# Rows gathered seven tiles ahead instead of three, and the eight PSUM buffers shared out anew

## The chip, the cores and the metric

The kernel runs on one core of one Trainium2 chip. The metric is the device time of one launch in microseconds (us); the median of three runs is given. The engines are PE (TensorE matmul), PEld (its weight loads), DVE (VectorE), ACT (ScalarE), POOL (GpSimd) and SP (SyncE, which here only starts DMAs). "Granted clock" is the share of full speed that PE was given: 1.00 is 2.4 GHz, 0.50 is 1.2 GHz.

## The reference

Linear attention with an RMS norm gives x (2304 tokens of 512), a top-1 mixture of eight experts follows, then a dense two-layer network.

```
kv = einsum('bhsd,bhse->bhde', k, v);  out = einsum('bhsd,bhde->bhse', q, kv)
x  = out / sqrt(mean(out*out) + 1e-6) * g_norm            # 2304 x 512
e  = argmax(x @ w_gate)                                   # one expert of 8 per token
y[token] = gate_w * (relu(x @ w1[e]) @ w2[e])             # 512 -> 1024 -> 512
h  = y @ w_in;  g = where(h > 0, h, exp(min(h, 0)) - 1);  out = g @ w_out   # 512 -> 2048 -> 512
```

## The kernel before, in words

The attention part writes the rows of x to a DRAM buffer (`x_dram`, 528 floats a row: 512 values and 16 scales), and works out `ids`, the order of the tokens sorted by expert. Experts are taken in rank order, the largest first; rank r works on a window of `WIN[r]` sorted tokens (352 for rank 0).

**Rows.** The sorted tokens form 18 tiles of 128 rows. For each tile a, POOL starts an indirect DMA (`gather`, line 494: 128 rows of 2112 bytes, 270 KB) into a row buffer `xg`; DVE scales the rows in place (`place_scale`, line 500); PE turns them with four 128x128 transposes into the PSUM tile `pt` (`place_turn`, line 507); ACT copies `pt` into `xT` (line 508). There are three row buffers (`XG = 3`), so the gather of tile a+3 is started behind the turn of tile a, and one `pt` buffer (`ps_x`).

**First window.** Tiles 0 to 2 are turned into the four `acc` buffers and become the split operands `xh`, `xl` of rank 0 at once (`first_window`, lines 561 to 571).

**Steps.** `step(u)` handles one eighth of an expert (8 steps a rank, 64 in all): it starts the weight loads of unit u+3 on SP (lines 532, 533, 256 KB each), runs the first-layer products h(u) (`expert_h`, 12 matmuls into `ph`, lines 587 to 589), then the second-layer products y(u-1) (`expert_y`, 12 matmuls into `acc`), and splits the weights of unit u+2 into a high and a low part (line 480 on ACT; line 483, in rank 0 `w1l` on POOL and `w2l` on DVE). From `ph`, ACT makes `hh` (line 606) and DVE `hl` (line 607).

Rank 0 also has to turn tiles 3 to 17, because rank 1 may start anywhere: `QUOTA[u]` tiles are turned in step u, one between h(u) and y(u-1), the others behind y(u-1); at step 5 all that are left are turned. Behind each step's turns `place_ahead(2)` scales the next two tiles. In steps 5 and 6 the window of rank 1 is made (`window`, lines 582, 583).

The program is issued in written order in this part (`tc.manual_schedule()`), so each engine's queue has the order of the code, and an instruction that waits holds up what stands behind it on its engine. `ps_h` holds the first-layer products `ph`, three buffers, in the expert part and in the dense network behind it (96 steps there: ACT reads `ph` twice over at lines 864 and 865, DVE makes `g` at line 867).

Of the kernel before, what the change touches and what calls it, by code (L numbers as in the profile page):

```python
# [9 lines left out]
F32 = mybir.dt.float32  # L10
# [7 lines left out]
PSUM = bass.MemoryType.PSUM  # L18
DRAM = bass.MemoryType.DRAM

P = 128
B, H, S, D = 4, 8, 576, 64
N, C = B * S, H * D
NT = N // P
# [17 lines left out]
def block_kernel(ctx, tc, qT, k, v, g_norm, w_gate, w1, w2, w_in, w_out, out, cap, **_):  # L42
    nc = tc.nc

    keep = ctx.enter_context(tc.tile_pool(name="keep", bufs=1))
    ids = keep.tile([P, NT], U32, name="ids")
# [7 lines left out]
    x_dram = dram.tile([N, C + 2 * H], F32, name="x_dram")  # L54
# [50 lines left out]
    with ExitStack() as actx:  # L105
# [30 lines left out]
        for b in range(B):  # L136
            t = ap1.tile([P, NP, KA], F32, name=f"kva{b}")
# [122 lines left out]
        def step(c, n=1):  # L260
            for _ in range(n):
                next(c)
# [200 lines left out]
    xw = ctx.enter_context(tc.tile_pool(name="xw", bufs=2, reuse_waits="tile"))  # L463
# [1 line left out]
    wst = ctx.enter_context(tc.tile_pool(name="wst", bufs=2, reuse_waits="tile"))  # L465
    ring = ctx.enter_context(tc.tile_pool(name="ring", bufs=7, reuse_waits="tile"))
    ps_a = ctx.enter_context(tc.tile_pool(name="ps_a", bufs=4, space=PSUM, reuse_waits="tile"))
    ps_h = ctx.enter_context(tc.tile_pool(name="ps_h", bufs=3, space=PSUM, reuse_waits="tile"))
    ps_x = ctx.enter_context(tc.tile_pool(name="ps_x", bufs=1, space=PSUM, reuse_waits="tile"))
    xctx = ExitStack()  # L470
    xp = xctx.enter_context(tc.tile_pool(name="xp", bufs=1, reuse_waits="tile"))
    xT = xp.tile([P, NP, NS], F32, name="xT")
# [12 lines left out]
    def ring_tiles():  # L485
        return [ring.tile([P, C], F32R, name=n) for n in ("w1h", "w1l", "w2h", "w2l")]

    XG = 3
    xg_t = {}

    def gather(a):
        if a < NT:
            xg_t[a] = wst.tile([P, C + 2 * H], F32, name="xg", tag="w64", bufs=XG)
            return nc.gpsimd.indirect_dma_start(out=xg_t[a], out_offset=None, in_=x_dram,
                                         in_offset=bass.IndirectOffsetOnAxis(ap=ids[:, a:a + 1], axis=0))

    def place_scale(a):
        xg = xg_t[a]
        v = xg[:, 0:C].rearrange("p (h d) -> p h d", h=H)
        nc.vector.scalar_tensor_tensor(out=v, in0=v, scalar=used[:, a:a + 1], in1=xg[:, C:C + H].to_broadcast([P, H, D]),  # L500
                                       op0=ALU.mult, op1=ALU.mult)

    def place_turn(a):
        xg = xg_t.pop(a)
        pt = ps_x.tile([P, NP, P], F32, name="pt")
        for j in range(NP):
            nc.tensor.transpose(pt[:, j], xg[:, j * P:(j + 1) * P], ident)
        nc.scalar.activation(xT[:, :, a * P:(a + 1) * P], pt, AF.Copy, scale=g_col)
        gather(a + XG)

    offs, eids = {}, {}

# [2 lines left out]
    def load_regs(r):  # L515
        with ExitStack() as behind:
            for i in mark.values():
                behind.enter_context(tc.issue_after(i.ins))
            eids[r] = reg(0, r, [SP_E], 0, E - 1)
            offs[r] = reg(1, r, [ACT_E, DVE_E], 0, off_max(r)) if r else 0  # L520
# [3 lines left out]
    def expert_load(u):  # L524
        if u >= NU:
            return
        r, fc = divmod(u, NF)
        if fc == 0:
            load_regs(r)
        a1 = wst.tile([P, C], F32, name="a1", tag="a", bufs=AB)  # L530
        a2 = wst.tile([P, C], F32, name="a2", tag="a", bufs=AB)
        first = nc.sync.dma_start(out=a1, in_=w1[bass.ds(eids[r], 1), fc].rearrange("o p c -> (o p) c"))
        mark["sp"] = nc.sync.dma_start(out=a2, in_=w2[bass.ds(eids[r], 1), fc].rearrange("o p c -> (o p) c"))
        wstage[u] = (a1, a2)
        return first

    def expert_split(u, engine=nc.gpsimd):
        if u >= NU:
            return
        w = ring_tiles()  # L540
        a1, a2 = wstage.pop(u)
        split_hi(w[0:2], a1)
        mark["act"] = split_hi(w[2:4], a2)
        split_lo(w[0:2], a1, engine)
        mark["dve"] = split_lo(w[2:4], a2, nc.vector)
        wtiles[u] = w
# [3 lines left out]
    def first_window():  # L550

        W = WIN[0]
        xh = xw.tile([P, NP, WIN[0]], F32R, name="xh")
        xl = xw.tile([P, NP, WIN[0]], F32R, name="xl")
        pts, ws = [], []
        for a in range(need[0]):
            place_scale(a)
            xg = xg_t.pop(a)
            pt = ps_a.tile([P, NP, P], F32, name="pt", tag="acc")
            for j in range(NP):  # L560
                nc.tensor.transpose(pt[:, j], xg[:, j * P:(j + 1) * P], ident)
            w = slice(a * P, min(W, (a + 1) * P))
            nc.scalar.activation(xh[:, :, w], pt[:, :, :w.stop - w.start], AF.Copy, scale=g_col)
            gather(a + XG)
            pts.append(pt)
            ws.append(w)
        for pt, w in zip(pts, ws):
            nc.vector.scalar_tensor_tensor(out=xl[:, :, w], in0=pt[:, :, :w.stop - w.start], scalar=g_col, in1=xh[:, :, w].bitcast(F32),
                                           op0=ALU.mult, op1=ALU.subtract)
        for a, pt in enumerate(pts):  # L570
            nc.scalar.activation(xT[:, :, a * P:(a + 1) * P], pt, AF.Copy, scale=g_col)
        xwin[0] = (xh, xl)
        placed["s"] = placed["t"] = need[0]
# [19 lines left out]
    def expert_h(u):  # L593
        r, fc = divmod(u, NF)
        W = WIN[r]
        w1h, w1l = wtiles[u][0:2]
        xh, xl = xwin[r]
        ph = ps_h.tile([P, C], F32, name="ph")

        for w in [slice(a, min(W, a + P)) for a in range(0, W, P)] if u < 0 else [slice(0, W)]:  # L600
            for j in range(NP):
                c = slice(j * P, (j + 1) * P)
                three(ph[:, w], (w1h[:, c], w1l[:, c]), (xh[:, j, w], xl[:, j, w]), j == 0, j == NP - 1)
        hh = hp.tile([P, WIN[0]], F32R, name="hh")
        hl = hp.tile([P, WIN[0]], F32R, name="hl")
        nc.scalar.activation(hh[:, :W], ph[:, :W], AF.Relu)  # L606
        nc.vector.scalar_tensor_tensor(out=hl[:, :W], in0=ph[:, :W], scalar=0.0, in1=hh[:, :W].bitcast(F32),
                                       op0=ALU.max, op1=ALU.subtract)
        hid[u] = (hh, hl)
# [25 lines left out]
    class Prep:  # L635
# [5 lines left out]
        def load(self):  # L641
            src = (w_in, w_out)[self.half][self.u]
            if wide:
                self.st = wst.tile([P, 2 * C], I32, name="w64", bufs=XG)
                nc.sync.dma_start(out=self.st, in_=src.bitcast(I32))
# [103 lines left out]
    def place_ahead(n):  # L749
        while placed["s"] < min(placed["t"] + n, NT):  # L750
            place_scale(placed["s"])
            placed["s"] += 1

    def place(n, ahead):

        while placed["t"] < min(n, NT):
            while placed["s"] < min(placed["t"] + 1, NT):
                place_scale(placed["s"])
                placed["s"] += 1
            place_turn(placed["t"])  # L760
            placed["t"] += 1
        place_ahead(ahead)
# [22 lines left out]
    APART = 4 * NF + 4  # L785
    FIRST = NF + 1

    QUOTA = (1, 2, 2, 3, 2, 2, 3, 0)

    def step(u):  # L790
        r, fc = divmod(u, NF)
# [6 lines left out]
        if u < NU:  # L798
            expert_h(u)
        q = QUOTA[u] if u < NF else 2 if more else 0  # L800
        if q:
# [23 lines left out]
    with tc.manual_schedule():  # L825
        expert_load(0)
        expert_load(1)
        gathers = [gather(a) for a in range(XG)]
        expert_split(0, nc.vector)
        expert_split(1, nc.vector)  # L830
        first_window()
        tc.add_manual_dep(expert_load(2).ins, gathers[1].ins.name, mybir.DependencyInfo(mybir.DependencyClass.Sync, mybir.DependencyReason.DATA),
                          reason="rows before weights")
        place_ahead(2)
        for u in range(APART + 1):
            mark.clear()
            step(u)
# [118 lines left out]
```

## Time and profile before

| | us |
|---|---|
| runs | 721.87, 724.04, 725.79 (median 724.04) |
| the profiled execution | 721.96 |
| its span, first to last instruction | 720.2 |
| PE busy | 692.4 (96%) |

The profiled execution is 2.1 us under the median of the runs, and 1.8 us of it lie outside the span. A row of a window gives its length and the busy time of each engine with the number of instructions in brackets, then the granted clock of PE, the busy share of the 16 DMA engines and what they moved. A row of the timeline gives start and duration in us, engine, source line, operation, output<-inputs, and in brackets how long the engine sat idle before it and what released it.

### The profile page before, as it was taken

What the parts mean: (1) busy time and instruction counts of PE and PEld (TensorE: products, weight loads), DVE (VectorE), ACT (ScalarE), POOL (GpSimd) and SP (SyncE); (2) the same over time, 40 slices, a digit from 0 to 9 for tenths busy, and PEclk for the clock granted to TensorE, in tenths of its full rate; (3) what the DMA queues carried; (4) which work ended last, traced back from release to release, by engine and by line L of the source; (5) the groups of instructions that cost most, each with busy time, mean ns of one, the idle gap of its engine ahead of it and who ended that gap; (6) DMA issues with size and microseconds to landing.
All of it is one profiled execution on the core that took longest, in us unless ns stands there. A gap on an engine that the chain in (4) does not pass through costs nothing.

```text
span 720.2 us, 11582 instructions
## 1 busy us (share of the span) xinstructions
PE 692.4 (96%) x4310; PEld 645.6 (90%) x4310; DVE 425.3 (59%) x789; ACT 347.8 (48%) x689; POOL 96.9 (13%) x108
## 2 busy tenths in 40 slices
PE   7997787999999999999999999999999999999996
PEld 6987787999998999999999998998999999899895
DVE  4567655767876878655555545666994334333342
ACT  1552554455555655566566554444654334333331
POOL 7121472000000000052222000000000000011122
PEclk9998798999999999999999999999999999999999
DMA  8995774556555657435335434333542223233312
GB/s 286 397 304 142 218 214 130 176 172 197 170 181 155 218 165 253 133 132 190 146 118 217 163 117 147 118 146 118 196 154 90 103 115 119 101 132 131 132 45 87
DMA packets 55423, 117.53 MB, mean 163 GB/s; under 512 B 8000, under 2 KB 21824, under 8 KB 55360
## 3 DMA queue, kind: packets, MB, share of 16 engines
q1 hardware_dynamic: 51744, 107.12, 43.8%
q0 software_dynamic: 2880, 9.59, 3.9%
q8 instruction: 36, 0.59, 0.3%
q14 instruction: 27, 0.22, 0.1%
q10 hardware_dynamic: 736, 0.02, 0.1%
HBM read 97.68 MB, written 19.02 MB: 162 GB/s over the span
## 4 chain that ended last, share of the span: by engine, by line
PE 59%; issue 8%; POOL 1%; POOLq 0%; DVE 0%
PE ph L587 10%; PE ph L589 10%; PE ph L588 10%; PE acc L887 8%; PE acc L888 8%; PE acc L886 8%; PE acc L589 2%; PE acc L587 2%; PE acc L588 2%; POOL out L897 1%; POOLq L952 0%; DVE part L894 0%; POOLq L897 0%
## 5 line engine op out<-in xcount | busy, mean ns | idle before, releaser
L867 DVE SCALAR_TENSOR_TENSOR g<-e,ph 128x384 f32<-128x384 f32 x96 | 53.0, 552 | 133.6 <-ACT e L865 133.3
L589 PE MATMUL ph<-yl,w1h 128*128 128x384 f32 x384 | 129.5, 337 | 0.0
L587 PE MATMUL ph<-yh,w1h 128*128 128x384 f32 x384 | 129.3, 337 | 0.0
L588 PE MATMUL ph<-yh,w1l 128*128 128x384 f32 x384 | 129.0, 336 | 0.0
L864 ACT ACTIVATE e<-ph 128x384 f32<-128x384 f32 x96 | 47.2, 492 | 160.8 <-PE ph L589 160.7
L888 PE MATMUL acc<-w2h,gl 128*128 128x512 f32 x288 | 114.0, 396 | 0.0
L887 PE MATMUL acc<-w2l,gh 128*128 128x512 f32 x288 | 113.7, 395 | 0.0
L886 PE MATMUL acc<-w2h,gh 128*128 128x512 f32 x288 | 112.0, 389 | 0.0
L587 PE MATMUL ph<-xh,w1h 128*128 128x288 f32 (+6 forms) x256 | 79.2, 309 | 2.4 <-PEq L734 1.7
L589 PE MATMUL ph<-xl,w1h 128*128 128x288 f32 (+6 forms) x256 | 78.5, 306 | 0.0
L588 PE MATMUL ph<-xh,w1l 128*128 128x288 f32 (+6 forms) x256 | 78.4, 306 | 0.0
L587 PE MATMUL acc<-hh,w2h 128*128 128x288 f32 (+6 forms) x256 | 77.5, 303 | 0.0
L588 PE MATMUL acc<-hh,w2l 128*128 128x288 f32 (+6 forms) x256 | 77.0, 301 | 0.0
L589 PE MATMUL acc<-hl,w2h 128*128 128x288 f32 (+6 forms) x256 | 76.9, 301 | 0.0
L587 PEld LDWEIGHTS ph<-yh,w1h 128*128 128x128 f32 x384 | 72.2, 188 | 4.2
L588 PEld LDWEIGHTS ph<-yh,w1l 128*128 128x128 f32 x384 | 72.1, 188 | 4.1
L589 PEld LDWEIGHTS ph<-yl,w1h 128*128 128x128 f32 x384 | 72.0, 188 | 0.0
L480 ACT ACTIVATE gh<-g 128x384 fp32r<-128x384 f32 x96 | 50.4, 525 | 43.1 <-DVE g L867 41.3
L483 DVE TENSOR_TENSOR gl<-g,gh 128x384 fp32r<-128x384 f32 x96 | 55.7, 580 | 18.1 <-ACT gh L480 18.1
L606 ACT ACTIVATE hh<-ph 128x288 fp32r<-128x288 f32 (+6 forms) x64 | 27.1, 423 | 81.0 <-PE ph L589 81.0
L888 PEld LDWEIGHTS acc<-w2h,gl 128*128 128x128 f32 x288 | 54.0, 187 | 11.6
L887 PEld LDWEIGHTS acc<-w2l,gh 128*128 128x128 f32 x288 | 54.0, 187 | 9.2
(157 smaller groups left out, 1188.1 us busy)
## 6 DMA issues: line engine op xcount, KB each, us to landing
a<-w SPq DMA_DIRECT2D x128, 256.0 KB
yh<-y_dram SPq DMA_DIRECT2D x18, 768.0 KB
yl<-y_dram SPq DMA_DIRECT2D x18, 768.0 KB
w<-w_in SPq DMA_DIRECT2D x16, 512.0 KB
w<-w_out SPq DMA_DIRECT2D x16, 512.0 KB
kt<-k SPq DMA_DIRECT2D x18, 256.0 KB
vt<-v SPq DMA_DIRECT2D x18, 256.0 KB
x_dram<-oz_all SPq DMA_DIRECT2D x18, 256.0 KB
```

What stands on the lines that cost most here:

```text
L480: return nc.scalar.activation(dst[0], src, AF.Copy)
L483: return engine.tensor_tensor(out=dst[1], in0=src, in1=dst[0].bitcast(F32), op=ALU.subtract)
L587: nc.tensor.matmul(out, lhsT=ah, rhs=bh, start=start, stop=False)
L588: nc.tensor.matmul(out, lhsT=al, rhs=bh, start=False, stop=False)
L589: nc.tensor.matmul(out, lhsT=ah, rhs=bl, start=False, stop=stop)
L606: nc.scalar.activation(hh[:, :W], ph[:, :W], AF.Relu)
L864: nc.scalar.activation(e, ph[:, :BT], AF.Relu, scale=-1.0)
L867: nc.vector.scalar_tensor_tensor(out=g, in0=e, scalar=-1.0, in1=ph[:, :BT], op0=ALU.add, op1=ALU.max)
L886: nc.tensor.matmul(acc, lhsT=gh[:, ts], rhs=w2h, start=(c == 0), stop=False)
L887: nc.tensor.matmul(acc, lhsT=gh[:, ts], rhs=w2l, start=False, stop=False)
L888: nc.tensor.matmul(acc, lhsT=gl[:, ts], rhs=w2h, start=False, stop=(c == NC2 - 1))
L897: put = nc.gpsimd.indirect_dma_start(out=out, out_offset=bass.IndirectOffsetOnAxis(ap=ids[:, i:i + 1], axis=0), in_=part[:, i], in_offset= ...
```

## The change

Seven gathers are started at once instead of three. Of each seven tiles, three go to the `xg` buffers as before and four into two tiles named `lent`, which take the first buffers of the pool tags `xh` and `xl`; those buffers are next used by the window of rank 1. The gather of tile a+7 is started behind the turn of tile a. `pt` gets two PSUM buffers, and `ph` two where it had three. Step 0 turns two tiles instead of one, step 3 two instead of three. The weight loads of unit 2 wait for the third gather instead of the second.

```
-    ps_h = ctx.enter_context(tc.tile_pool(name="ps_h", bufs=3, space=PSUM, reuse_waits="tile"))
-    ps_x = ctx.enter_context(tc.tile_pool(name="ps_x", bufs=1, space=PSUM, reuse_waits="tile"))
+    ps_h = ctx.enter_context(tc.tile_pool(name="ps_h", bufs=2, space=PSUM, reuse_waits="tile"))
+    ps_x = ctx.enter_context(tc.tile_pool(name="ps_x", bufs=2, space=PSUM, reuse_waits="tile"))
...
-    XG = 3
+    XG, XE = 3, 4
     xg_t = {}
...
+    def gather():
+
+        a = gathered["n"]
+        if a >= NT:
+            return
+        gathered["n"] += 1
+        k = a % (XG + XE)
+        if k >= XG:
+            xg_t[a] = lent[k - XG]
+        else:
             xg_t[a] = wst.tile([P, C + 2 * H], F32, name="xg", tag="w64", bufs=XG)
...
-        gather(a + XG)
+        gather()
...
-    QUOTA = (1, 2, 2, 3, 2, 2, 3, 0)
+    QUOTA = (2, 2, 2, 2, 2, 2, 3, 0)
...
-        gathers = [gather(a) for a in range(XG)]
+        for tag in ("xh", "xl"):
+            t = xw.tile([P, XE // 2, C + 2 * H], F32, name="lent", tag=tag)
+            lent.extend(t[:, n] for n in range(XE // 2))
+        gathers = [gather() for _ in range(XG + XE)]
...
-        tc.add_manual_dep(expert_load(2).ins, gathers[1].ins.name, mybir.DependencyInfo(mybir.DependencyClass.Sync, mybir.DependencyReason.DATA),
+        tc.add_manual_dep(expert_load(2).ins, gathers[2].ins.name, mybir.DependencyInfo(mybir.DependencyClass.Sync, mybir.DependencyReason.DATA),
```

POOL's queue at the start of the expert part, before (x7 is seven gathers in a row, in program order: three at once, three of the first window, one of step 0; `w1l` is the weight split):

```order
L494 DMA xg<-x_dram,ids 128x528 x7
L483 TENSOR_TENSOR w1l<-a_1022,w1h 128x512
L494 DMA xg<-x_dram,ids 128x528 x2
L483 TENSOR_TENSOR w1l<-a_1028,w1h 128x512
L494 DMA xg<-x_dram,ids 128x528 x2
L483 TENSOR_TENSOR w1l<-a_1066,w1h 128x512
L494 DMA xg<-x_dram,ids 128x528 x3
```

The same place now:

```order
L504 DMA xg<-x_dram,ids 128x528 x3
L504 DMA lent<-x_dram,ids 128x528 x4
L504 DMA xg<-x_dram,ids 128x528 x3
L504 DMA lent<-x_dram,ids 128x528 x2
L483 TENSOR_TENSOR w1l<-a_1028,w1h 128x512
L504 DMA lent<-x_dram,ids 128x528 x2
L483 TENSOR_TENSOR w1l<-a_1034,w1h 128x512
L504 DMA xg<-x_dram,ids 128x528 x2
```

Twelve gathers instead of seven stand ahead of the first weight split on POOL.

PE's queue in step 3, between y(2) and h(4), before (numbers tell the tiles apart; `pt` are turned rows):

```order
L507 MATMUL pt_1229<-ident_63,xg_1156 128x128 x4
L507 MATMUL pt_1238<-ident_63,xg_1176 128x128 x4
L587 MATMUL ph_1261<-xh_987,w1h_1180 128x352
L588 MATMUL ph_1261<-xh_987,w1l_1181 128x352
L589 MATMUL ph_1261<-xl_988,w1h_1180 128x352
```

and now:

```order
L599 MATMUL acc_1110<-hl_1158,w2h_1073 128x352
L517 MATMUL pt_1240<-ident_63,lent_965 128x128 x4
L597 MATMUL ph_1262<-xh_993,w1h_1191 128x352
L598 MATMUL ph_1262<-xh_993,w1l_1192 128x352
L599 MATMUL ph_1262<-xl_994,w1h_1191 128x352
```

One turn has left this place; it stands in step 0 now, behind h(0) and the turn that was there.

## Rows read from the trace of the kernel before

**Rows 1.** The page, busy time of each engine over the span.
```profile
PE 692.4 (96%) x4310; PEld 645.6 (90%) x4310; DVE 425.3 (59%) x789; ACT 347.8 (48%) x689; POOL 96.9 (13%) x108
```
**Rows 2.** Windows by step: busy us (instructions) per engine, PEclk, DMA share, GB/s.
```profile
78.11:81.86 3.75, 3.75 (x12) 3.35 (x12) 0.78 (x2) 1.68 (x3) 1.13 (x2) 0.50 0.99 363
81.86:85.28 3.42, 2.95 (x18) 2.77 (x18) 2.10 (x4) 2.18 (x4) 1.37 (x2) 0.79 0.20 77
...
90.00:94.72 4.72, 4.72 (x34) 4.68 (x33) 2.45 (x4) 2.86 (x6) 3.32 (x4) 1.00 0.81 249
94.72:100.87 6.15, 5.37 (x37) 4.98 (x35) 3.20 (x4) 3.53 (x6) 4.77 (x5) 1.00 0.78 216
100.87:107.11 6.24, 4.90 (x34) 4.74 (x34) 3.45 (x5) 2.88 (x6) 4.54 (x5) 1.00 0.64 196
107.11:116.65 9.54, 5.47 (x33) 4.60 (x32) 4.39 (x6) 3.19 (x6) 3.04 (x3) 0.86 0.50 140
116.65:122.48 5.83, 5.83 (x26) 5.83 (x25) 3.04 (x4) 4.30 (x8) 2.15 (x2) 0.64 0.29 90
122.48:126.31 3.83, 3.83 (x26) 3.83 (x25) 2.46 (x4) 1.74 (x4) 1.04 (x2) 1.00 0.57 169
126.31:720.00 593.69, 586.13 (x3374) 547.91 (x3372) 350.35 (x631) 293.57 (x586) 45.06 (x43) 1.00 0.42 147
```
**Rows 3.** What PE waited for, 78.11 to 720: us in total, times, longest.
```profile
PE pt L507 <- DVE xg L500: 4.3, 3, 2.5
PE ph L587 <- PEq L734: 1.7, 1, 1.7
PE pt L507 <- ACT xT L508: 1.6, 2, 0.8
PE pt L507 <- issue: 0.8, 1, 0.8
```
**Rows 4.** Timeline of PE: turns with idle time ahead of them.
```profile
102.36 0.63 PE L507 MATMUL pt<-ident,xg 128*128 128x128 f32 x4 [1.34 <-DVE xg L500]
...
109.47 0.60 PE L507 MATMUL pt<-ident,xg 128*128 128x128 f32 x4
...
110.85 0.66 PE L507 MATMUL pt<-ident,xg 128*128 128x128 f32 x4 [0.78 <-ACT xT L508]
...
114.02 1.08 PE L507 MATMUL pt<-ident,xg 128*128 128x128 f32 x4 [2.52 <-DVE xg L500]
...
115.89 1.11 PE L507 MATMUL pt<-ident,xg 128*128 128x128 f32 x4 [0.78 <-ACT xT L508]
```
**Rows 5.** Timeline of POOL: gathers of tiles 2, 3, 16 and 17.
```profile
71.59 0.95 POOL L494 DMA_INDIRECT xg<-x_dram,ids  x1 [0.30 <-issue]
76.00 1.02 POOL L494 DMA_INDIRECT xg<-x_dram,ids  x1 [3.46 <-PE pt L561]
...
108.12 1.24 POOL L494 DMA_INDIRECT xg<-x_dram,ids  x1 [0.16 <-issue]
110.34 0.94 POOL L494 DMA_INDIRECT xg<-x_dram,ids  x1 [0.98 <-PE pt L507]
```
**Rows 6.** Timeline of DVE: the scaling of tiles 2, 3, 16 and 17.
```profile
75.45 0.75 DVE L500 SCALAR_TENSOR_TENSOR xg<-xg,used 128x512 f32<-128x512 f32 x1 [0.24 <-DMA xg<-x_dram,ids]
...
81.68 0.75 DVE L500 SCALAR_TENSOR_TENSOR xg<-xg,used 128x512 f32<-128x512 f32 x1 [2.97 <-DMA xg<-x_dram,ids]
...
113.17 0.75 DVE L500 SCALAR_TENSOR_TENSOR xg<-xg,used 128x512 f32<-128x512 f32 x1 [2.96 <-DMA xg<-x_dram,ids]
114.52 0.75 DVE L500 SCALAR_TENSOR_TENSOR xg<-xg,used 128x512 f32<-128x512 f32 x1 [0.60 <-DMA xg<-x_dram,ids]
```
**Rows 7.** Timeline of SP: the first weight load of unit 2.
```profile
74.07 0.33 SPq L532 DMA_DIRECT2D a<-w  x1
```
**Rows 8.** Timeline of ACT: the split of unit 2, the copy of tile 16.
```profile
84.15 0.62 ACT L480 ACTIVATE w1h<-a 128x512 fp32r<-128x512 f32 x1
...
115.14 0.69 ACT L508 ACTIVATE xT<-pt,g_col 128x512 f32<-128x512 f32 x1 [2.91 <-PE pt L507]
```
**Rows 9.** Dense network, timeline of DVE: `g` of its step 0.
```profile
315.59 0.55 DVE L867 SCALAR_TENSOR_TENSOR g<-e,ph 128x384 f32<-128x384 f32 x1 [2.67 <-ACT e L865]
```
**Rows 10.** Dense network, timeline of PE: the start of its step 2.
```profile
316.39 0.33 PE L587 MATMUL ph<-yh,w1h 128*128 128x384 f32 x1
```

More of the change, by code (lines that the diff above doesn't have):

```diff
@@ L486, in ring_tiles @@
         return [ring.tile([P, C], F32R, name=n) for n in ("w1h", "w1l", "w2h", "w2l")]
-    XG = 3
+    XG, XE = 3, 4
     xg_t = {}
-    def gather(a):
-        if a < NT:
+    lent = []
+    gathered = {"n": 0}
+    def gather():
[7 more added lines that the diff above has]
+        else:
             xg_t[a] = wst.tile([P, C + 2 * H], F32, name="xg", tag="w64", bufs=XG)
-            return nc.gpsimd.indirect_dma_start(out=xg_t[a], out_offset=None, in_=x_dram,
-                                         in_offset=bass.IndirectOffsetOnAxis(ap=ids[:, a:a + 1], axis=0))
+        return nc.gpsimd.indirect_dma_start(out=xg_t[a], out_offset=None, in_=x_dram,
+                                            in_offset=bass.IndirectOffsetOnAxis(ap=ids[:, a:a + 1], axis=0))
     def place_scale(a):
@@ L563, in first_window @@
             nc.scalar.activation(xh[:, :, w], pt[:, :, :w.stop - w.start], AF.Copy, scale=g_col)
-            gather(a + XG)
+            gather()
             pts.append(pt)
```

## The prediction

> **What bounds the kernel now.** PE is busy for 96% of the span, the next engine, DVE, for 59% [rows 1], so a change is worth what it does to PE's idle time and to PE's clock. I read the windows first, cut where PE ends h(1), h(2) and so on [rows 2]. From 126.31 us to the end PE is busy for 586.13 of 593.69 us; of the rest 1.7 us is one wait behind a branch [rows 3] and the other six lie at the very end, behind the last matmul. Nothing but PE's own work sets that part, so a microsecond won before 126.31 is a microsecond off the end, and the change must earn its time between 78.11 and 126.31, in rank 0.
>
> There the same windows show what a step costs without stalls. h(7) and y(6), with no turn, take 3.83 us. A step with two turns takes 4.72 us with PE never idle (the step from 85.28 to 90.00 is equal to the one shown), so one turn costs (4.72 - 3.83) / 2 = 0.44 us. The next steps are longer: 6.15 (three turns, 0.78 idle), 6.24 (two turns, 1.34 idle) and 9.54 us for the stretch from the end of h(5) to h(6), which holds y(4) and five turns and where PE is busy for 5.47 us only. Then h(6) and y(5) take 5.83 us where the pair behind them takes 3.83, at a granted clock of 0.64 against 1.00.
>
> The waits say what PE lacks: `xg` scaled by DVE, 4.3 us in three waits, the longest 2.5 [rows 3]. DVE is not slow; it waits for the gather [rows 6]. From the start of a gather on POOL to its scaling it takes 75.45 - 71.59 = 3.9 us (tile 2), 81.68 - 76.00 = 5.7 (tile 3), 113.17 - 108.12 = 5.1 (tile 16) and 114.52 - 110.34 = 4.2 (tile 17) [rows 5, 6]. With three buffers a gather starts behind the turn of the tile three before, and is scaled two turns before its own, so it has one turn's distance, half a step or 2.4 us, to land. It is late every time, and the steps that turn more run the store of rows empty. The second wait is for ACT to empty the only `pt`, 1.6 us in two waits [rows 3, 4]. The clock follows: it is 1.00 up to an idle stretch of 2.52 us at 111.5, which comes 0.78 us of idling after the turn before, and the turn at 114.02 takes 1.08 us where the one at 109.47 took 0.60; the idle 1.34 us before 102.36 did not lower it [rows 2, 4].
>
> **The change, part by part.** *Gathers seven ahead.* A gather now starts behind the turn of the tile seven before, five turns before its scaling: 2.5 steps, 11.8 us, against the 3.9 to 5.7 us that it takes. The first seven start in one run on POOL. At the spacing of a gather and its gap (0.95 + 0.30) [rows 5] tile 6 starts 4 x 1.25 = 5.0 us behind tile 2, at 76.6, and can be scaled at 80.5 to 82.3; DVE comes to it behind `hl` of h(0) and tile 5, about 83.5 to 84. So tiles 3 to 6 wait for nothing, and the later ones have 11.8 us. Twelve gathers stand ahead of POOL's first weight split instead of seven; the last two of them wait for the turns of step 0, which end by 83.5, so the split of unit 2 starts near 85.5, and h(2) asks for it at about 88. Hidden; without that cover each microsecond would be PE's.
>
> *Weights of unit 2 behind the third gather.* Their load starts at 74.07 [rows 7]; it moves to the landing of tile 2, about 75.4 [rows 6]. ACT splits them at 84.15 [rows 8], 8.7 us later: hidden. In the same time the gathers of tiles 3 to 9 (seven of 270 KB, 1.9 MB) and the loads of units 2 to 4 (1.57 MB) want the DMA engines: 3.46 MB, 9.5 us at the 363 GB/s of the window from 78.11, 13.9 us at the 249 GB/s of the one from 90.00 [rows 2]. The Trainium skill (DMA: Bandwidth & Descriptors, Issuing engines are not separate DMA queues) speaks against the change here: DMAs of different issuers share the same 16 DMA engines and interleave, so early rows are paid for by late weights. By that rule and equal shares, unit 2 (0.52 MB) would land behind some 1.05 MB. In time, at 249 GB/s, 1.05 MB are 4.2 us, so unit 2 is there at 79.6, 4.5 us before ACT asks. Even were it served last of all, at 75.4 + 9.5 = 84.9 to 89.3, PE's h(2) would wait for 0 to 3 us. I take 0. In the steady steps two gathers and one unit are 1.06 MB in 4.72 us, 225 GB/s, less than the 249 moved in the window where PE was never idle.
>
> *Step 0 and step 3.* One turn moves from step 3 to step 0, where the clock is still 0.50 up to about 83.3 [rows 2]. There it costs 0.4 to 0.9 us and the idle 0.47 (3.42 - 2.95) goes: 81.86 to 85.28 becomes 3.4 to 3.85 us, I take 3.6, so h(1) ends at 85.5 instead of 85.28.
>
> *Four steps with two turns each.* They take 4.72 each if the rows are there: 18.9 us where the four took 4.72 + 4.72 + 6.15 + 6.24 = 21.8. h(5) ends at 104.4 instead of 107.11.
>
> *Step 5.* One turn (0.44), y(4) (1.92, half of 3.83) and four turns in a row. With two `pt` PE can turn while ACT copies, so their pace is that of the slowest of PE (0.44), ACT's copy (0.69) [rows 8] and DVE's scaling (0.75) [rows 6], which for the last three tiles stands in this place. 0.44 + 1.92 + 0.44 + 3 x 0.75 = 5.05 us instead of 9.54. Bounds: all four at 0.44 gives 4.1; all at the pace of one buffer, 110.85 - 109.47 = 1.38, gives 7.9. With the rows long there I stay at 5.05.
>
> *Clock.* PE would have gaps of 0.3 us between those turns instead of 2.52; gaps of 1.34 left the clock at 1.00. So h(6) and y(5) take 3.83, not 5.83. They start earlier, and ACT and DVE must follow: behind the copy of tile 17 ACT has two splits and half of rank 1's window, about 2 us, before `hh` of h(6). That is as long as h(6), so `hh` may come half a microsecond late; y(6) needs it a whole y(5) later. Hidden.
>
> *Two `ph`.* Each h now waits for the readers of the h two before. In rank 0 to 7 a whole step lies between. In the dense network 59 first matmuls get a wait for DVE. The tightest is h of step 2: `g` of step 0 ends at 315.59 + 0.55 = 316.14 and that h starts at 316.39 [rows 9, 10], 0.25 us to spare; from then on a second-layer group of 2 us stands between, and the spare is over 2 us. Price 0, up to 0.3 at that one place.
>
> *`lent`.* Its space is next written by rank 1's window, which reads all 18 turned tiles anyway; no new wait. The wait behind the branch (1.7 us) may move by its own size either way.
>
> **The sum.** h(7) starts at 104.4 + 5.05 + 3.83 = 113.3 instead of 122.48: 9.2 us less. The profiled execution would take 721.96 - 9.2 = 712.8 us; it lies 2.1 under the median, so against the median of the runs 724.04 - 9.2 = 714.8, say **715 us**.
>
> **Rivals.** *The clock falls all the same* in the four turns, or they go at the old pace. The falling clock costs 5.83 - 3.83 = 2.0 and 0.45 for each of two turns, 2.9 us: 718. For it: PE would be idle for a third of these 2.7 us. Against it: at 98 to 102 us PE was idle for longer, and nothing fell.
>
> *The DMA engines are the limit*, and the rows or weights come late again. If they give only the 196 to 216 GB/s of the windows with stalls [rows 2], 1.06 MB take 4.9 to 5.4 us, 0.2 to 0.7 more a step, up to 3 us over five steps, and with one fall of the clock (2.9) up to 6: 717 to 721. Against it: those windows moved little because gathers were not started, not because they queued.
>
> *Nothing changes*: the stall moves to ACT, DVE or POOL in the same steps, 724. In the fully busy step DVE has 2.45, ACT 2.86 and POOL 3.32 of 4.72 us [rows 2], so there is room for all three.
>
> *Slower*: the waits on two `ph`. If each of the 59 cost PE 0.16 us, they would eat the whole 9.2; at 0.22 the kernel is over 0.5% slower, 728. That needs `g` to be over 2 us later than in the trace, 58 times.
>
> **Chances.** The forecast 0.66; clock or pace 0.13; DMA limit 0.10; no change 0.05; slower 0.06. About 0.5% (3.6 us, to 720.4) is what a measurement of this kernel tells from no change: faster takes the first two and most of the third, 0.86; same 0.08; slower 0.06. The range: the forecast alone 712 to 717.5 (step 5 between 4.1 and 7.9, the branch wait, 2 us of spread between runs); with the clock and most of the DMA cases it is 711.5 to 720.
>
> **What would show it.** PE without idle time from 78 to about 106.7; no wait of DVE for gathered rows behind tile 2; four turns in 2.7 us; the granted clock 1.00 from about 83.3 to the end; h(7) at 113.3. Wrong would be: PE waiting for `w1l` of unit 2, DVE still waiting for DMA `xg` or `lent`, a second stretch at 0.50, or PE waiting for `g` in the dense network.

## The result

The changed kernel takes **714.41 us** (median of four runs, 713.83 to 715.01) against 723.35 us for the kernel before on the same chip; the ratio is 0.9869, 95% interval 0.9843 to 0.9894. The forecast was 715 us with 9.2 us less; 8.9 us less were measured. The profiled execution took 713.83 us, its span 712.0.

The busy line of the page after, which answers to [rows 1]: PE's work is the same, in a shorter span.

```profile
PE 691.2 (97%) x4310; PEld 645.4 (91%) x4310; DVE 426.5 (60%) x789; ACT 347.4 (49%) x689; POOL 99.0 (14%) x108
```

The windows of the kernel after, cut at the same places as [rows 2], and behind them the stretch at the branch behind step 36, from the last product of y(35) to the end of h(37):

```profile
77.50:81.26 3.76, 3.75 (x13) 3.54 (x14) 2.03 (x3) 1.69 (x3) 2.84 (x4) 0.50 1.01 369
81.26:84.59 3.33, 3.33 (x22) 3.31 (x21) 1.94 (x3) 2.71 (x5) 2.41 (x3) 0.84 1.04 412
...
89.31:94.03 4.72, 4.72 (x34) 4.68 (x33) 3.65 (x4) 2.86 (x6) 4.08 (x5) 1.00 0.89 278
94.03:98.73 4.70, 4.70 (x34) 4.66 (x33) 3.39 (x4) 2.85 (x6) 3.80 (x4) 1.00 0.82 249
98.73:103.44 4.71, 4.71 (x34) 4.67 (x33) 3.13 (x4) 2.86 (x6) 2.46 (x3) 1.00 0.61 185
103.44:108.16 4.72, 4.38 (x33) 3.96 (x32) 3.77 (x5) 2.70 (x6) 0.85 (x1) 1.00 0.35 111
108.16:112.07 3.91, 3.91 (x27) 3.91 (x26) 1.86 (x2) 3.91 (x8) 1.59 (x2) 1.00 0.05 3
112.07:115.90 3.83, 3.83 (x26) 3.83 (x25) 3.36 (x6) 2.31 (x5) 2.03 (x2) 1.00 0.78 246
...
216.17:218.90 2.73, 0.29 (x4) 0.09 (x2) 1.06 (x2) 0.26 (x1) 0.00 (x0) 1.00 0.03 9
218.90:221.92 3.02, 3.02 (x13) 3.02 (x14) 0.00 (x0) 0.00 (x0) 0.00 (x0) 0.50 0.65 184
```

The reader should see three things. Each of the four steps takes 4.72 us or a hair less, where two took 6.15 and 6.24. The stretch with five turns takes 4.72 instead of 9.54 us, and h(6) with y(5) behind it 3.91 instead of 5.83, at a granted clock of 1.00. And at the branch PE stands for 2.4 us and then runs h(37) at 0.50, in 3.02 us, which the first profile of before does not show: h(37) took 1.66 us there, at 1.00, from 228.60 to 230.26, where y(36) starts.

```profile
228.60 0.37 PE L587 MATMUL ph<-xh,w1h 128*128 128x288 f32 x1 [1.73 <-PEq L734]
...
230.26 0.30 PE L587 MATMUL acc<-hh,w2h 128*128 128x288 f32 x1
```

What PE waited for in the kernel after, from 66 us on, beside [rows 3]: the first wait lies ahead of the first window, where the kernel before waits 3.9 us too. The 4.3 us for scaled rows behind it are gone, and the wait for the copied tile has shrunk from 1.6 to 0.3. The line of 2.4 us is the branch.

```profile
PE pt L571 <- DVE xg L510: 4.0, 1, 4.0
PE ph L597 <- PEq L744: 2.4, 1, 2.4
PE ph L597 <- ACT xh L573: 0.7, 1, 0.7
PE pt L517 <- ACT xT L518: 0.3, 1, 0.3
```

PE's timeline at the end of step 5, which answers to [rows 4]: four turns from 105.79 to the first product of h(6) at 108.16, 2.4 us with 0.34 idle.

```profile
105.79 1.03 PE L517 MATMUL pt<-ident,xg 128*128 128x128 f32 x8
107.17 0.66 PE L517 MATMUL pt<-ident,xg 128*128 128x128 f32 x4 [0.34 <-ACT xT L518]
107.75 0.66 PE L517 MATMUL pt<-ident,lent 128*128 128x128 f32 x4
108.16 0.40 PE L597 MATMUL ph<-xh,w1h 128*128 128x352 f32 x1
```

The gather of tile 6 on POOL and the weight split of unit 2 behind the twelve gathers; then, on DVE, the scaling of tiles 4 and 6, the only ones of the borrowed buffers that still waited for rows. They answer to [rows 5, 6].

```profile
76.80 0.95 POOL L504 DMA_INDIRECT lent<-x_dram,ids  x1 [0.31 <-DVE xl L578]
...
85.42 1.30 POOL L483 TENSOR_TENSOR w1l<-a,w1h 128x512 fp32r<-128x512 f32 x1
```

```profile
79.13 0.75 DVE L510 SCALAR_TENSOR_TENSOR lent<-lent,used 128x512 f32<-128x512 f32 x1 [0.35 <-DMA lent<-x_dram,ids]
...
83.82 0.75 DVE L510 SCALAR_TENSOR_TENSOR lent<-lent,used 128x512 f32<-128x512 f32 x1 [0.64 <-DMA lent<-x_dram,ids]
```

Where the time came from is read from ACT, which makes `hh` behind each h and `e` behind each first-layer product of the dense network. Of the kernel after, `hh` of h(0) and of h(8), and the first `e`:

```profile
81.50 0.47 ACT L616 ACTIVATE hh<-ph 128x352 fp32r<-128x352 f32 x1 [2.31 <-PE ph L599]
...
117.95 0.45 ACT L616 ACTIVATE hh<-ph 128x336 fp32r<-128x336 f32 x1 [2.26 <-PE ph L599]
...
306.33 0.49 ACT L877 ACTIVATE e<-ph 128x384 f32<-128x384 f32 x1 [2.00 <-PE ph L599]
```

The same three before:

```profile
82.10 0.47 ACT L606 ACTIVATE hh<-ph 128x352 fp32r<-128x352 f32 x1 [2.31 <-PE ph L589]
...
128.36 0.45 ACT L606 ACTIVATE hh<-ph 128x336 fp32r<-128x336 f32 x1 [2.26 <-PE ph L589]
...
314.50 0.49 ACT L864 ACTIVATE e<-ph 128x384 f32<-128x384 f32 x1 [2.00 <-PE ph L589]
```

From the first `hh` to the second are 36.45 us, before 46.26. So rank 0 gave 9.8 us in these two profiles; by the windows, 3.0 of it are in the four steps with two turns, 4.8 in the stretch with five, and 1.9 in h(6) and y(5), where the clock no longer falls. The part ahead of it came out 0.6 us earlier, and the part from `hh` of h(8) to the first `e` of the dense network took 188.38 instead of 186.14 us, 2.2 more, all at the branch (the runs without the branch, below, show that). The rest, 405.7 us, is the same to 0.03 us. 9.8 + 0.6 - 2.2 = 8.2 us, the difference of the spans.

### The profile page after: what moved, and what is told of

Its sections match the earlier page's. It is cut to its first block, busy times and chain, and to the rows that moved or that the text cites. A ratio compares the mean times of both kernels' runs of the same rounds, so it can differ in the third digit from the quotient of the medians.

```text
span 712.0 us, 11591 instructions
## 1 busy us (share of the span) xinstructions
PE 691.2 (97%) x4310; PEld 645.4 (91%) x4310; DVE 426.5 (60%) x789; ACT 347.4 (49%) x689; POOL 99.0 (14%) x108
## 4 chain that ended last, share of the span: by engine, by line
issue 44%; PE 22%; POOL 2%; POOLq 0%; ACT 0%
PE ph L597 4%; PE ph L598 4%; PE ph L599 4%; PE acc L597 2%; PE acc L599 2%; PE acc L598 2%; POOL out L910 2%; PE acc L900 1%; PE acc L901 1%; PE acc L899 1%; POOL yl L483 1%; POOLq L965 0%; ACT yh L480 0%; ACT e L877 0%; POOLq L910 0%
```

## The experiments

Theory: a gather must start early enough to land before its tile is scaled; that lead earns the time, and the second buffer for turned rows matters only once the rows are there. Rivals: the second turned buffer earns it by itself; the number of gathers in flight at the start does; the lost 2.2 us are the change's own doing.

All runs in one table. The two segments come from each run's profile, as above: "rank 0" from `hh` of h(0) to `hh` of h(8), "branch" from there to the first `e` of the dense network. The runs lie on several chips, so the ratio, taken against the kernel before on the same chip, is what compares.

| kernel | us | ratio (95%) | rank 0 | branch |
|---|---|---|---|---|
| before | 723.35 | 1 | 46.26 | 186.14 |
| before again | 723.15 | 0.9999 (0.9975 to 1.0022) | 44.68 | 187.99 |
| buffers only | 723.94 | 0.9993 (0.9978 to 1.0008) | 45.24 | 188.10 |
| four ahead | 719.35 | 0.9925 (0.9907 to 0.9942) | 40.91 | 188.12 |
| seven ahead, old buffers | 718.72 | 0.9922 (0.9896 to 0.9947) | 39.71 | 188.60 |
| five ahead | 716.54 | 0.9883 (0.9865 to 0.9901) | 36.94 | 188.29 |
| the changed kernel | 714.41 | 0.9869 (0.9843 to 0.9894) | 36.45 | 188.38 |
| the changed kernel again | 714.84 | 0.9883 (0.9863 to 0.9903) | 37.06 | 188.02 |
| changed, old spread of turns | 714.87 | 0.9883 (0.9858 to 0.9907) | 37.11 | 188.21 |
| changed, loads behind gather 2 | 714.47 | 0.9882 (0.9859 to 0.9906) | 36.83 | 188.24 |
| before, no branch | 720.27 | 0.9957 (0.9941 to 0.9974) | 46.22 | 184.19 |
| changed, no branch | 710.34 | 0.9822 (0.9806 to 0.9839) | 36.58 | 184.19 |
| changed, long fill | 715.39 | 0.9897 (0.9880 to 0.9915) | 35.94 | 188.05 |
| changed, short fill | 713.71 | 0.9868 (0.9842 to 0.9893) | 36.02 | 188.22 |

**The buffers alone**, in the kernel before.

```
-    ps_h = ctx.enter_context(tc.tile_pool(name="ps_h", bufs=3, space=PSUM, reuse_waits="tile"))
-    ps_x = ctx.enter_context(tc.tile_pool(name="ps_x", bufs=1, space=PSUM, reuse_waits="tile"))
+    ps_h = ctx.enter_context(tc.tile_pool(name="ps_h", bufs=2, space=PSUM, reuse_waits="tile"))
+    ps_x = ctx.enter_context(tc.tile_pool(name="ps_x", bufs=2, space=PSUM, reuse_waits="tile"))
```

> The kernel before with only the PSUM buffers moved: two for turned rows, two for first-layer products; rows still gathered three ahead. Theory (rows that start earlier earn the time): the turns still wait for gathered rows, and only part of the 1.6 us that PE waited for the copy of the one turned tile can go: 0 to 1.6 us less than the kernel before, 722 to 723.5 us, and the clock still falls around 114 us. Rival (the second buffer for turned rows earns it): 5 us or more less, 718 us or below.

No difference, ratio 0.9993, as the theory has it. PE's turns at the end of step 5 wait for rows, not for the copied tile, and the last runs at the low clock:

```profile
109.93 0.63 PE L507 MATMUL pt<-ident,xg 128*128 128x128 f32 x4 [1.33 <-DVE xg L500]
111.48 0.63 PE L507 MATMUL pt<-ident,xg 128*128 128x128 f32 x4 [0.93 <-DVE xg L500]
113.67 1.09 PE L507 MATMUL pt<-ident,xg 128*128 128x128 f32 x4 [1.56 <-DVE xg L500]
```

This run also prices the two `ph`: from the first `e` of the dense network to the end it takes 405.72 us against 405.70, so the 59 new waits cost nothing there.

**Seven ahead with the old buffers**, in the changed kernel.

```
-    ps_h = ctx.enter_context(tc.tile_pool(name="ps_h", bufs=2, space=PSUM, reuse_waits="tile"))
-    ps_x = ctx.enter_context(tc.tile_pool(name="ps_x", bufs=2, space=PSUM, reuse_waits="tile"))
+    ps_h = ctx.enter_context(tc.tile_pool(name="ps_h", bufs=3, space=PSUM, reuse_waits="tile"))
+    ps_x = ctx.enter_context(tc.tile_pool(name="ps_x", bufs=1, space=PSUM, reuse_waits="tile"))
```

> The changed kernel with the PSUM buffers of before (one for turned rows, three for first-layer products); rows seven ahead. Theory: the four turns in a row go at the pace of one buffer, 1.38 instead of some 0.75 us, three times, and the second turn of step 0 waits once: 2 to 2.5 us more than the changed kernel, 716.5 to 717 us; the clock does not fall around 107 us. Rival (the buffers earn it): 720 us or more.

Ratio 0.9922, 5.8 us under that chip's kernel before (724.52); expected was 716.5 to 717, it came at 718.7. Rank 0 takes 39.71, 2.7 to 3.3 more than with two turned buffers; the turns behind each other come every 1.4 us, as one buffer allows, and never wait for rows:

```profile
109.89 0.66 PE L517 MATMUL pt<-ident,xg 128*128 128x128 f32 x4 [0.78 <-ACT xT L518]
111.33 0.66 PE L517 MATMUL pt<-ident,xg 128*128 128x128 f32 x4 [0.78 <-ACT xT L518]
112.76 0.66 PE L517 MATMUL pt<-ident,lent 128*128 128x128 f32 x4 [0.78 <-ACT xT L518]
```

So the second buffer is worth nothing without the rows and about 3 us with them. The granted clock is 1.00 from 107 to 115 us, although three idle pieces of 0.78 us lie between the turns.

**Five and four ahead**, in the changed kernel (`XE` is 2, then 1).

```
-    XG, XE = 3, 4
+    XG, XE = 3, 2
...
-        for tag in ("xh", "xl"):
-            t = xw.tile([P, XE // 2, C + 2 * H], F32, name="lent", tag=tag)
-            lent.extend(t[:, n] for n in range(XE // 2))
+        for tag in ("xh",):
+            t = xw.tile([P, XE, C + 2 * H], F32, name="lent", tag=tag)
+            lent.extend(t[:, n] for n in range(XE))
```

> The changed kernel with rows five ahead (two borrowed buffers instead of four). A gather starts three turns, 1.5 steps or 7.1 us, before its scaling, and takes 3.9 to 5.7 us in the trace of before. Theory (the lead over the landing time decides): as fast as seven ahead, 714.4 us within 1. Rival (a store of rows is needed because the DMA engines cannot keep up): 2 us or more slower, 716.5 us or above.

> The changed kernel with rows four ahead (one borrowed buffer). The lead is two turns, one step or 4.7 us, in the middle of the 3.9 to 5.7 us that a gather takes. Theory: most tiles are just in time or up to 1 us late, and the four turns in a row find one tile late: 716 to 719 us. Rival (what counts is the number in flight at the start): close to the kernel before, 721 us or above.

Five ahead is as good as seven: its ratio, 0.9883, is that of the changed kernel's second measurement, and rank 0 takes 36.94 us. (Its 716.54 us lie above the 714.4 within 1 that I had named, and at the rival's bound; that chip's kernel before ran at 724.5, 8.0 us above it, so the ratio and the segment decide here.) Four ahead gives 0.9925. In its steps with two turns no turn waits for rows; what fails is the row of four turns, where the lead is two turns in quick succession. DVE waits 2.39 us for the last tile's rows, PE 2.50, and the clock falls as in the kernel before:

```profile
111.92 0.75 DVE L510 SCALAR_TENSOR_TENSOR xg<-xg,used 128x512 f32<-128x512 f32 x1 [2.39 <-DMA xg<-x_dram,ids]
```

```profile
112.78 1.08 PE L517 MATMUL pt<-ident,xg 128*128 128x128 f32 x4 [2.50 <-DVE xg L510]
```

So the lead decides, and what is enough here lies between two turns and three.

**The changed kernel again.** The same text, for a control beside the next runs.

> The changed kernel once more, as it is, beside the next three on one chip. Theory: 714.4 us within 1, and a second profile shows rank 0's steps as in the first (33.2 us from hh of h(1) to hh of h(8)), whatever the part ahead of them does. Rival: the first four runs were a lucky draw and it comes at 716 us or more, as rows five ahead did.

714.84 us. Rank 0 takes 37.06; from `hh` of h(1) on it is 33.17 in both profiles. The start differs: `hh` of h(0) comes at 83.38 here and at 81.50 in the first, and 1.7 of these 1.9 us lie ahead of all that the change touches, since the first gather starts at 69.99 here and at 68.33 there.

**Without the branch.** The second pass, which these inputs skip, is left out of both kernels.

```
-            beyond_windows()
```

> The kernel before without the second pass for tokens beyond an expert's window, and so without its branch. The branch costs PE 2 us of waiting, and in some executions the clock falls behind it, 2 us more. Theory: 2 to 4 us less than the kernel before, 720 to 722 us. Rival: the wait is covered, no difference.

> The changed kernel without that second pass. Theory (the 2.2 us that the profile after loses behind the branch are a draw, not a result of the change): 2.5 to 4.5 us less than the changed kernel, 710 to 712 us, and the distance to the kernel before without the branch is 9 to 10.5 us, about as with it. Rival (the change makes the branch dearer): that distance grows to 11 us or more.

Before falls by 2.8 us to 720.27, the changed kernel by 4.5 to 710.34; the distance is 9.9 us, near the 9.6 that rank 0 gives in these two profiles, and both take 184.19 us in the segment with the branch gone. So the whole 2.2 us of the first two profiles lie at the branch, and none of it elsewhere. With the branch the distance on this chip is 8.2 us (723.05 against 714.84); it did not grow to the rival's 11, but it is not the same either.

**The kernel before again.**

> The kernel before once more, for a second profile. If the fall of the clock behind the branch is a draw, it shows here too or not, whatever the change does: 184.2 + 2 us from hh of h(8) to the dense network without it, some 188 us with it. The steps of rank 0 from hh of h(0) to hh of h(8) take 46.2 us as in the first profile.

Here the clock falls behind the branch too, only a little later; the second matmul row below is one of y(36) and takes 0.44 instead of 0.29 us. The segment takes 187.99 us.

```profile
227.72 0.37 PE L587 MATMUL ph<-xh,w1h 128*128 128x288 f32 x1 [2.03 <-PEq L734]
...
229.50 0.44 PE L587 MATMUL acc<-hh,w2h 128*128 128x288 f32 x1
```

So the clock can fall there without the change; the first profile of before is the one that escaped. Rank 0 took 44.68 instead of 46.26 us here, which the expectation had not foreseen. The waits fall differently from run to run: PE waits for scaled rows 4.4 us in four pieces, the longest 1.5, where the first profile has 4.3 in three, the longest 2.5, and 1.1 us for the copied tile instead of 1.6.

**The old spread of the turns, and the loads behind the second gather**, each alone in the changed kernel (the second: `gathers[1]` for `gathers[2]` in the line that makes the loads wait).

```
-    QUOTA = (2, 2, 2, 2, 2, 2, 3, 0)
+    QUOTA = (1, 2, 2, 3, 2, 2, 3, 0)
```

> The changed kernel with the old spread of the turns (one in step 0, three in step 3). Theory (the spread only moves one turn): the same within 1 us, 714 to 715.5 us; one turn leaves the stretch at 1.2 GHz, at most 0.5 us less. Rival (the spread is needed so that rows are used as they land): 2 us or more slower.

> The changed kernel with the weight loads of unit 2 behind the second gather, as before the change. Theory (the weights of unit 2 are there 4 us before ACT asks, and the third tile lands before the loads are under way): the same within 1 us. Rival (loads and rows compete for the DMA engines): h(0) starts later, 1 to 2 us slower.

0.9883 and 0.9882: neither shows a difference. Their intervals leave some 1.8 us either way, but rank 0, at 37.11 and 36.83 us, lies as in the changed kernel's own two profiles or within 0.1 us of them.

**Matmuls in the first wait.** PE waits 4.0 us for the first rows, and the granted clock is 0.50 in h(0) behind it. Extra matmuls of the identity fill that wait, 32 and then 14 of them.

```
+        idle = ps_x.tile([P, NP, P], F32, name="idle", tag="pt")
+        for _ in range(32):
+            nc.tensor.matmul(idle[:, 0], lhsT=ident, rhs=ident, start=True, stop=True)
         first_window()
```

> The changed kernel with 32 extra matmuls of the identity on PE (into an unused PSUM tile, results not read) in the 4 us in which PE waits for the first rows. Theory (that idle stretch lowers the clock for the first turns and h(0)): the granted clock stays at 1.00 through h(0), which takes 1.9 instead of 3.75 us; first turns, h(0) and the turns behind it win 2.5 to 3 us, of which up to 1.5 us may be lost again to rows 5 and 6, on which DVE already waits 0.6 us: 711.5 to 713.5 us. Rival (the clock is no loss there, since the rows set the pace): 714 us, no difference.

It came at 715.39 us, not at 711.5 to 713.5. I had not seen that each of these matmuls takes two passes: the trace has 64 rows for the 32, they last 7.3 us and end at 78.85, 4.1 us behind the first scaled tile. (The other two tiles were scaled only at 78.34 in this profile, so not all of the delay is the fill's.) The clock part of the theory holds, though. In the long fill the first turns take 1.47 instead of 2.46 us and h(0) runs at the full clock:

```profile
71.54 7.31 PE L846 MATMUL idle<-ident 128*128 128x128 f32 x64
78.68 1.47 PE L571 MATMUL pt<-ident,xg 128*128 128x128 f32 x12
81.90 0.43 PE L597 MATMUL ph<-xh,w1h 128*128 128x352 f32 x1 [1.74 <-ACT xh L573]
83.09 0.32 PE L597 MATMUL ph<-xh,w1h 128*128 128x352 f32 x1
```

> The changed kernel with 14 extra identity matmuls instead of 32 (each takes two passes of 0.114 us, so 3.2 us instead of 7.3, which ends before the first scaled rows). Theory (the idle stretch lowers the clock for the first turns and h(0)): the twelve first turns take 1.5 instead of 2.4 us, h(0) 1.9 instead of 3.75 us, 2 to 3 us less than the changed kernel, 712 to 713 us. Rival (the rows set the pace there): 714 to 715 us, no difference.

The short fill ran at 712.02 to 717.12 us, median 713.71 where 712 to 713 was expected, ratio 0.9868, against 0.9869 and 0.9883 of the changed kernel: 1 us better at most, and not told apart by these runs. Its profile is of the execution of 717.12 us: there ACT stood still for 2.9 us ahead of the third copy of the first window, PE for 5.2, and the clock fell after all. Nothing of the kernel's own is named as what released ACT, and the cause is not settled; so whether a fill of the right length pays stays open.

```profile
80.76 0.58 ACT L573 ACTIVATE xh<-pt,g_col 128x384 fp32r<-128x384 f32 x1 [2.86 <-remote]
```

## Why the prediction was right

**Rows seven ahead: right.** The four steps with two turns take 18.85 us, 18.9 was forecast, and DVE waits for gathered rows 1.0 us in all instead of 13.9 between 66 and 125 us. Mis-sized was the landing of the first gathers: tile 6 starts at 76.80 as forecast (76.6) but can be scaled only at 83.82, 7.0 us later, not 3.9 to 5.7. The DMA engines are full there, 369 and 412 GB/s from 77.50 to 84.59. So one of the prediction's signs of being wrong did show, DVE still waiting for `lent`; it cost PE nothing, since PE turns that tile at 86.95.

**Weights of unit 2 behind the third gather: right.** Their load starts at 75.01 (75.4 forecast), and ACT splits them at 83.51 with no wait in its row:

```profile
75.01 0.33 SPq L542 DMA_DIRECT2D a<-w  x1
```

```profile
83.51 0.63 ACT L480 ACTIVATE w1h<-a 128x512 fp32r<-128x512 f32 x1
```

What came late in these microseconds was a gather, that of tile 6, and undoing this edit (the loads behind the second gather) showed no difference. By the rule of the Trainium skill that the prediction named (DMA: Bandwidth & Descriptors, Issuing engines are not separate DMA queues), transfers of different issuers interleave on the same 16 engines. The 369 and 412 GB/s with a late gather fit that, but the prediction's reading of it, that the weights would pay, did not come true.

**Twelve gathers ahead of the weight split on POOL: right.** It starts at 85.42 (85.5) and ends at 86.72; h(2) starts at 87.31, not at about 88, so 0.6 us of the cover were left.

**Step 0: slightly too dear.** 3.33 us instead of 3.6 with the turn that was added.

**Step 5: right, a little too dear.** 4.72 us against 5.05. DVE began its last three scalings at 105.19, 0.6 us ahead of the four turns, so it did not set the pace; ACT's copy ended the only idle piece, 0.34 us.

**Clock: right at the place forecast**, 3.91 us for h(6) and y(5) (3.83 forecast) at 1.00. What the prediction missed was the other place: it had 1.00 to the end, and named a second stretch at 0.50 as a sign of being wrong, which the branch then showed. It had said that the wait behind the branch may move by its own size either way; the wait did grow (2.44 against 1.73 us), but the clock that falls behind it costs 1.4 us more, which no row of the first profile showed.

**Two `ph`: right**, no cost.

**The sum.** In the first two profiles rank 0 gave 9.8 us against 9.2, the part ahead 0.6, and the branch took 2.2 back, 8.2 in all; the medians show 8.9. Single profiles move by more than these differences: over the three profiles of each kernel, those without the branch among them, rank 0 takes 45.7 us before and 36.7 after, 9.0 less. The forecast of 715 us was right for the reason named, the rows, the second `pt` and the clock in rank 0. That it came within 0.6 us is in part luck, since what the branch takes back was in no term of the sum. How often the clock falls at the branch in either kernel is open: all nine profiles of kernels with the branch and rows four or more ahead show it, two of the three with rows three ahead. The medians without the branch put up to 1.7 us more on it in the changed kernel (4.5 against 2.8), within their intervals; why the change should make it dearer, if it does, no run shows.

## What to carry to other kernels

Count how long before its use a transfer is started, in time, and compare it with what it takes from issue to use under load. A lead just too short still leaves the longest stalls where the uses crowd (four ahead), and buffers beyond a lead that is enough bring nothing more (seven ahead against five). Where two resources limit the same place, the second can show no gain until the first is lifted, as `pt` did here, so try them together and apart. A wait that ends at a lower clock costs more than its length: read the windows behind it, too.

## What the runs showed of the hardware

The branch that PE takes over a skipped body of code held it for 2.0 to 2.9 us, from the start of the last product to the start of the next, although its condition was loaded at 214.4 us in the changed kernel, 1.8 us ahead of that last product. PE's row of the branch lasts 3996 ns there, and those of SP, ACT, DVE and POOL 45 to 72 ns.

```profile
L744 PEldq COMPARE_BRANCH  x1: 3996/3996/3996, 214.5 to 214.5; - x1
```

The Trainium skill (Runtime: NRT & Kernel Launch, Instruction fetch mechanics) says that a taken branch to code that is not yet at hand stalls for a fetch. The trace agrees as far as it goes: it has DMA packets of the kind "instruction", eight of them between 215.8 and 220.7 us, where the changed kernel without the branch has none between 211.6 and 222.4. Over the whole span the two queues of that kind carry these packets, first with the branch, then without:

```profile
q8 instruction: 36, 0.59, 0.3%
q14 instruction: 27, 0.22, 0.1%
...
q8 instruction: 34, 0.56, 0.3%
q14 instruction: 22, 0.18, 0.1%
```

The trace does not name the engine that these packets are for, so that PE's wait is for one of them is not shown.

A gather of 270 KB took 3.7 to 7.0 us from its issue to its landing, median 4.3, for the nine into the borrowed buffers of the changed kernel:

```profile
DMA to landing us min/median/max: 3.7/4.3/7.0
```

PE's granted clock stayed at 1.00 through an idle piece of 1.34 us (before), and through three of 0.78 with turns between (seven ahead, old buffers). It fell to 0.50 after 2.50 us (four ahead) and 2.52 us (before) ahead of a turn, after 1.33, 0.93 and 1.56 us close together (buffers only), and at the branch after waits of 2.0 us and more in eleven profiles, but not after the one of 1.73 (before).
